# First DFT stage in float32 instead of split F32R, and the biases as one wide product

## The chip, the cores and the metric

The kernel runs on one core of a Trainium2 chip. The metric is the device time of one execution in microseconds. TensorE (PE) does the matrix products, with its weight loads shown as an engine of their own (PEld); VectorE (DVE), ScalarE (ACT) and GpSimd (POOL) do the elementwise work; SyncE (SP) issues the DMAs.

## The reference

The input x is 8 x 3072 x 256. A real Fourier transform over the 3072 positions is followed by a complex linear layer with biases, a soft threshold of 0.01 and the inverse transform; then a two-layer MLP and a routed layer of experts.

```python
X = np.fft.rfft(x, axis=1)                      # 3072 = 96 x 32
Xr, Xi = X.real, X.imag
Yr = Xr @ w_r - Xi @ w_i + b_r
Yi = Xr @ w_i + Xi @ w_r + b_i
Y  = soft(Yr, 0.01) + 1j * soft(Yi, 0.01)
y  = np.fft.irfft(Y, n=3072, axis=1)
h  = np.maximum(y @ w_in, 0.0)                  # 256 -> 2048
z  = h * h @ w_out                              # 2048 -> 256
# softmax routing of the 24576 tokens to 32 slots, 8 experts, and back
```

## The kernel before

The kernel has three parts: the spectrum (transform, linear layer, threshold and the first half of the inverse transform), some 600 us; the MLP with the second half of the inverse transform and the routing beside it, nearly all of the rest; and the experts with the recombination, the last 200 us. Products that need more precision than one F32R product gives split both factors into an upper part and a remainder and add three F32R products (`mm3`, L127 to L130: upper by upper L128, upper by lower L129, lower by upper L130).

The transform is done as 96 x 32. The first stage (`a_...`) multiplies by the 96 x 96 matrix `f1t`. Its input is loaded in tiles `xt` of 96 x 4 x 256 (`load_x`, L193, 64 in all, `XB` of them at a time). A half tile j (512 columns, 16 per batch, 128 in all) is cast to its upper part `xh` by ScalarE (`a_hi`, L199), its remainder `xl` is taken by VectorE (`a_lo`, L204; four of the first 16 by GpSimd), and `a_mm` adds three products in a bank psA. `a_out` (L222) copies the bank to `sa`, and one DMA for each tile stores it in `ad` in DRAM (L224). `load_b` (L231) reads it back as `bt` for two units.

A unit u (12 per batch, 96 in all) is one step of the rest: `b_mm` (second transform stage, four float32 products of 128 columns into psB, L239), `b_hi`, `b_lo` and `b_sum` (upper parts, remainders and the sum `Sf` of real and imaginary part), `l_mm` (linear layer), `l_move`, `l_relu` and `l_soft` (the bank read out and the threshold), `c_mm` (first inverse stage, two float32 products of 256 columns into psC, L321) and `c_out` (copy and four stores to `zd`, L327 to L331). `l_mm` fills one bank psL: for the real and the imaginary half (256 columns each) two `mm3` of 128 x 128 by 256 columns, and then one bias product, which closes that half's sum:

```python
nc.tensor.matmul(p[:, c], lhsT=sel[:, c + (c and first)], rhs=bias, start=False, stop=True)   # L290
```

`bias` is 64 x 256 with b_i and b_r in rows 0 and 1 and their remainders in rows 32 and 33, all else zero; `sel` (64 x 3 x 128) selects the row for the half. In the first unit of a batch the imaginary half has two more `mm3`. Then two `mm3` of the common part fill a bank psS.

The order is written by hand: the loop runs over half steps h, two per unit, and the steps of several units lie in each half step, so that every engine's queue has a fixed order. In an even half step TensorE gets `b_mm(U)`, `l_mm(U-2)` and then a first-stage product; in an odd one `c_mm(U-4)` and then a first-stage product. One half tile is taken in each of the first 20 half steps and in two of three afterwards, until the batches are through (from some 506 us on there are none). `a_mm(j-2)`, `a_hi(j)`, `a_lo(j-1)` and `a_out(j-3)` belong to the same half step. All PSUM banks of this part are one pool of eight, taken in turn (`pbank`). The decoding of the MLP's weights takes a step in each half step on VectorE, ScalarE and GpSimd. All loads and stores of this part are issued on SP's queue in program order.

The first batch's 16 half tiles run alone in an opening; its stores, the constants and the loads of the first units follow, and the units begin at 32 us.

Of the kernel before, what the change touches and what calls it, by code (L numbers as in the profile page):

```python
# [10 lines left out]
F32 = mybir.dt.float32  # L11
# [22 lines left out]
def shape_constants():  # L34
    """DFT factors and selection matrices: they depend on the shapes alone.

    n = 32 n1 + n2, k = k1 + 96 k2.  A row k1 of a real first-stage spectrum is
    held as (c, h, p): c = re / im, k1 = p + 24 h; the im row of k1 = 0 holds
    the real row k1 = 48.  The second stage keeps, for k >= 1536, the conjugate.
    """  # L40
# [38 lines left out]
    # rows n2 = 8 t + c of a first inverse stage, kept as (c, t)  # L79
# [15 lines left out]
    # which of the rows (b_i, b_r; 32 on: their lower parts) goes where: real part, imaginary part, the  # L95
    # latter where slot 0 holds the real k = 1536
    sel = np.zeros((64, 3, 128))
    for r in (0, 32):
        sel[r + 1, 0] = 1.0
        sel[r, 1] = 1.0  # L100
        sel[r, 2, 1:] = 1.0
        sel[r + 1, 2, 0] = 1.0
# [12 lines left out]
def fft_moe_kernel(ctx, tc, x, w_r, w_i, b_r, b_i, moe_w_in, moe_w_out, moe2_phi, moe2_w1, moe2_w2,  # L115
# [39 lines left out]
    # Both MLP products are cut in pairs of 128 hidden units.  The first takes 7 products of blocks in  # L155
    # place of 8 (Strassen's in Winograd's form): A = w_in^T of a pair, B = two blocks of tokens.
# [7 lines left out]
    f1t = k1p.tile([N1, 2, N1], F32R, tag="f1t", name="f1t")  # L164
    f1h, f1l = f1t[:, 0], f1t[:, 1]
    bm = k1p.tile([128, NP, 128], F32, tag="bm", name="bm")
    cm = k1p.tile([128, NP, 128], F32, tag="cm", name="cm")
    # w_r, -(w_r + w_i), w_i - w_r
    lwh = [k1p.tile([128, 2, DM], F32R, tag=f"lwh{j}", name=f"lwh{j}") for j in range(3)]
    lwl = [k1p.tile([128, 2, DM], F32R, tag=f"lwl{j}", name=f"lwl{j}") for j in range(3)]  # L170
    bias = k1p.tile([64, DM], F32R, tag="bias", name="bias")
    sel = k1p.tile([64, 3, 128], F32R, tag="sel", name="sel")
# [6 lines left out]
    # ---------------- spectrum, complex linear layer, shrinkage, half of the way back: all batches  # L179
# [16 lines left out]
    def a_hi(j):  # L196
        load_x(j // 2)
        xh = wka.tile([N1, 2, DM], F32R, tag="xh", name=f"xh{j}", bufs=XS)
        nc.scalar.copy(xh, xt[j // 2][:, 2 * (j % 2):2 * (j % 2) + 2])  # L199
        xs[j] = [xh]  # L200

    def a_lo(j, eng):
        xl = wka.tile([N1, 2, DM], F32R, tag="xl", name=f"xl{j}", bufs=XS - 1)
        eng.tensor_tensor(out=xl, in0=xt[j // 2][:, 2 * (j % 2):2 * (j % 2) + 2], in1=f(xs[j][0]), op=ALU.subtract)  # L204
        if j % 2:
            xt.pop(j // 2)
            load_x(j // 2 + XB)
        xs[j].append(xl)

    def a_mm(j):  # L210
        if j % NA == 0:
            ad[j // NA] = dram.tile([N1, N2, DM], F32, tag="ad", name=f"ad{j // NA}", bufs=3)
        xh, xl = xs.pop(j)
        p = pbank(f"psA{j}")[:N1].rearrange("p (a d) -> p a d", a=2)
        mm3(p, f1h, f1l, xh, xl, True, True)
        pa[j] = p
# [34 lines left out]
    def b_lo(u):  # L251
        p = pb.pop(u)
        xh, xi = xb.pop(u)
        xl = wkb.tile([128, 2, 2, 128], F32R, tag="Xl", name=f"Xl{u}")
        sf = wkb.tile([128, 2, 128], F32, tag="Sf", name=f"Sf{u}", bufs=1)
        nc.vector.tensor_tensor(out=xl, in0=p, in1=f(xh), op=ALU.subtract)
        nc.vector.tensor_tensor(out=sf, in0=p[:, :, 0], in1=xi, op=ALU.add)
        if u % NU == 0:
            # k = 0 and k = 1536 share a slot: both are real
            dd = wkb.tile([128, 2, 1], F32, tag="dd", name=f"dd{u}")  # L260
            nc.vector.tensor_tensor(out=dd, in0=xi[:, :, 0:1], in1=p[:, :, 0, 0:1], op=ALU.subtract)
            nc.vector.tensor_copy(d0h[:, :, 0:1], dd)
            nc.vector.tensor_tensor(out=d0l[:, :, 0:1], in0=dd, in1=f(d0h[:, :, 0:1]), op=ALU.subtract)
            nc.vector.tensor_copy(sf[:, :, 0:1], p[:, :, 0, 0:1])
            nc.vector.tensor_copy(xh[:, :, :, 0:1], zero)
            nc.vector.tensor_copy(xl[:, :, :, 0:1], zero)
        sp[u] = [xh, xl, sf]
# [8 lines left out]
    def l_mm(u):  # L276
        """X_im times -(w_r + w_i) for the real part, X_re times w_i - w_r for the other; both with the biases.

        Then what the two share, (X_re + X_im) w_r.
        """  # L280
        xh, xl, h, l = sp.pop(u)
        first = u % NU == 0
        p = pbank(f"psL{u}").rearrange("p (c d) -> p c d", c=2)
        for c in range(2):
            for dh in range(2):
                mm3(p[:, c], xh[:, dh, 1 - c], xl[:, dh, 1 - c], lwh[1 + c][:, dh], lwl[1 + c][:, dh], dh == 0, False)
            if c == 1 and first:
                for dh in range(2):
                    mm3(p[:, c], d0h[:, dh], d0l[:, dh], lwh[0][:, dh], lwl[0][:, dh], False, False)
            nc.tensor.matmul(p[:, c], lhsT=sel[:, c + (c and first)], rhs=bias, start=False, stop=True)  # L290
# [5 lines left out]
    def l_move(u):  # L296
        """Slots (l, h, k2) x (c, d) to (c, h, k2) x (l, d)."""
# [35 lines left out]
    # the MLP's weights: float64 decoded to float32 from its bits, then parts of 12 bits  # L333
# [5 lines left out]
    def decode():  # L339
        """The weights of a pair of hidden tiles at a time; yields after a few instructions."""  # L340
# [13 lines left out]
        for n, (k, q, a) in enumerate(keys):  # L354
# [4 lines left out]
            if wide:  # L359
# [7 lines left out]
                # +-2^e; 1 + the fraction's upper 20 bits; its other 32 bits  # L367
# [23 lines left out]
            # A11, A12, S4, -A22; S1, S2, S3  # L391
# [14 lines left out]
    # ---------------- rest of the way back, MLP, routing of tokens  # L406
# [10 lines left out]
    def stage_d(s, bank):  # L417
        """B11, B21, B12, B22 of two blocks of tokens and the sums of these that the products take."""
# [41 lines left out]
    XB, XS, XL, SA = 5, 5, NC, 4  # L460
    with tc.manual_schedule():
# [4 lines left out]
        f1f = wka.tile([N1, N1], F32, tag="f1f", name="f1f", bufs=1)  # L466
        nc.sync.dma_start(f1f, c_f1)
        for j in range(XB):
            load_x(j)
        split(f1h, f1l, f1f)  # L470
        w_ri = [wka.tile([128, 2, DM], F32, tag=f"wri{k}", name=f"wri{k}", bufs=1) for k in range(2)]
        bs = wka.tile([2, DM], F32, tag="bs", name="bs", bufs=1)
        sf = wka.tile([64, 3, 128], F32, tag="sf", name="sf", bufs=1)
        for j in range(NA + 4):
            if j < NA:
                a_hi(j)
                a_lo(j, nc.gpsimd if j in (2, 5, 8, 11) else nc.vector)
            if 1 <= j <= NA:
                a_mm(j - 1)
            if j >= 4:  # L480
                a_out(j - 4, nc.scalar.copy if j % 2 else nc.vector.tensor_copy)
            if j == NA - 4:
                for t, v in zip(w_ri, (w_r, w_i)):
                    nc.sync.dma_start(t, v.rearrange("(a p) n -> p a n", p=128))
                nc.sync.dma_start(bs[0:1], b_i.rearrange("(o n) -> o n", o=1))
                nc.sync.dma_start(bs[1:2], b_r.rearrange("(o n) -> o n", o=1))
                nc.sync.dma_start(sf, c_se)
# [4 lines left out]
        nc.vector.tensor_copy(bias, zero[:64, 0, 0].broadcast_to([64, DM]))  # L492
# [7 lines left out]
        nc.scalar.copy(bias[0:2], bs)  # L500
        nc.vector.tensor_tensor(out=bias[32:34], in0=bs, in1=f(bias[0:2]), op=ALU.subtract)
# [6 lines left out]
        XB, XS, XL, SA = 2, 3, NB * NC, 2  # L508
# [17 lines left out]
        for h in range(2 * NT + 12):  # L526
            U, o = divmod(h, 2)
            # the first stage of the batches to come
            j = -1
            if (h < 20 or (h + 1) * 2 // 3 > h * 2 // 3) and aj < NB * NA + 3:  # L530
                j, aj = aj, aj + 1
            def first_stage():
                if NA <= j - 2 < NB * NA:
                    a_mm(j - 2)
                if NA <= j < NB * NA:
                    a_hi(j)
                if j >= NA + 3:
                    a_out(j - 3, nc.scalar.copy)

            if o == 0:  # L540
# [3 lines left out]
                if NA <= j - 1 < NB * NA:  # L544
                    a_lo(j - 1, nc.vector)
# [4 lines left out]
            else:  # L550
                at(U - 4, c_mm)
                at(U - 2, l_move)
                if NA <= j - 1 < NB * NA:
                    a_lo(j - 1, nc.vector)
# [52 lines left out]
        class Unit:  # L607
            """A pair of hidden tiles for two blocks of tokens."""
# [7 lines left out]
            def product(self, p, j, start):  # L616
                """One of the seven, on its own or onto a sum that may have been read."""
# [7 lines left out]
            def copy(self, tag):  # L625
                """What the sum of products holds so far."""
# [14 lines left out]
            def hi(self, k):  # L641
                """The upper part of the square: of the square, or from what was cut at zero."""
# [22 lines left out]
            def second(self, k):  # L665
                """Hidden tile k // 2 of the pair, block k % 2 of the tokens."""
# [18 lines left out]
        def small(shape, tag, i):  # L685
            """The last block's route runs beside the one before it, and takes what tokens no longer need."""
# [81 lines left out]
        # the experts' weights go where those of the MLP were  # L768
# [30 lines left out]
        # the softmax over tokens, from the parts that the partitions hold  # L799
# [30 lines left out]
        # what goes beside the products: slots of a superblock at which each of these takes a step  # L830
# [91 lines left out]
    # ---------------- slots through the experts, tokens from the slots  # L922
    with ExitStack() as p3:
# [12 lines left out]
        # how the tokens combine the slots: 8 blocks at a time, in two parts  # L936
# [93 lines left out]
def device_arrays(inputs):  # L1030
    """The inputs as they come; a float64 array as its raw bits."""
# [24 lines left out]
```

## Time and profile before

| | us |
|---|---|
| median of 3 runs | 2992.5 (2991.92 to 2994.35) |
| span of the profiled execution, first to last instruction | 2989.6 |
| what the median has beyond that span | 2.9 |
| TensorE busy | 2946.6 (99%) |
| VectorE busy | 2271.9 (76%) |
| ScalarE busy | 1787.9 (60%) |
| GpSimd busy | 241.4 (8%) |

The page gives the span of the profiled execution and not its device time. A matmul is pipelined and its end is modelled, so its slot is read from its start to the start of the next one, not from its length. L12 is line 12 of the kernel. A row of the timeline merges neighbours of one kind (x4: four instructions). A program's float32 product can show as more than one record.

### The profile page before, as it was taken

How to read it: one execution, taken by the hardware profiler on the slowest of the kernel's cores; microseconds unless marked ns; L12 is line 12 of the kernel's file. 1: busy time of each engine (PE TensorE's matmuls, PEld its weight loads, DVE VectorE, ACT ScalarE, POOL GpSimd, SP SyncE). 2: the span in 40 equal slices, each digit the busy share in tenths (PEclk: the TensorE clock that was granted, in tenths of full speed). 3: DMA queues.
4: the chain of work that ended last, by engine and by line, in shares of the span. 5: the costliest groups of instructions: out<-in, count | busy, mean ns of one | idle time of the engine just before them, and what ended most of it. 6: DMA issues, size and time to landing. Idle time of an engine off the chain costs nothing.

```text
span 2989.6 us, 50050 instructions
## 1 busy us (share of the span) xinstructions
PE 2946.6 (99%) x18382; PEld 2752.5 (92%) x18382; DVE 2271.9 (76%) x5077; ACT 1787.9 (60%) x4137; POOL 241.4 (8%) x274
## 2 busy tenths in 40 slices
PE   7999999999999999999999999999999999999988
PEld 5888888899999999999999999999999999999967
DVE  6888888677777777777777777777777777777745
ACT  5777777555555555565555656555555555555532
POOL 1344344100000000000000000000000000000021
PEclk9999999999999999999999999999999999999999
DMA  8777766310000000000000000000000000000269
GB/s 247 205 203 197 202 196 182 93 33 11 15 16 14 17 14 12 14 12 14 11 14 12 14 12 14 12 14 14 12 14 17 14 14 17 12 14 1 74 213 325
DMA packets 125737, 189.85 MB, mean 64 GB/s; under 512 B 15346, under 2 KB 98100, under 8 KB 125236
## 3 DMA queue, kind: packets, MB, share of 16 engines
q1 hardware_dynamic: 123700, 183.51, 21.2%
q10 hardware_dynamic: 1792, 3.15, 0.4%
q8 instruction: 145, 2.38, 0.3%
q14 instruction: 100, 0.82, 0.1%
HBM read 107.95 MB, written 78.64 MB: 62 GB/s over the span
## 4 chain that ended last, share of the span: by engine, by line
PE 94%; DMA 2%; DVE 2%; ACT 1%; SPq 1%; issue 1%; POOL 0%; ACTq 0%; POOLq 0%; DVEq 0%
PE psA L622 18%; PE psX L622 13%; PE psO L130 12%; PE psO L129 12%; PE psO L128 12%; PE psY L427 4%; PE psB L239 3%; PE psC L321 3%; PE psL L128 2%; PE psL L290 2%; PE psL L129 1%; PE psL L130 1%; PE psS L128 1%; PE pz L756 1%; PE pl L702 1%; PE psA L129 1%
## 5 line engine op out<-in xcount | busy, mean ns | idle before, releaser
L130 PE MATMUL psO<-gh,wo 128*128 128x384 f32 x2048 | 685.6, 335 | 0.0
L129 PE MATMUL psO<-gl,wo 128*128 128x384 f32 x2048 | 684.7, 334 | 0.0
L128 PE MATMUL psO<-gh,wo 128*128 128x384 f32 x2048 | 684.7, 334 | 0.0
L662 DVE TENSOR_TENSOR gl<-g,gh 128x384 fp32r<-128x384 f32 x1024 | 554.9, 551 | 77.4 <-ACT gh L645 73.4
L645 ACT CAST gh<-g 128x384 fp32r<-128x384 f32 x512 | 263.4, 515 | 401.9 <-DVE g L654 400.6
L129 PEld LDWEIGHTS psO<-gl,wo 128*128 128x128 f32 x2048 | 384.5, 188 | 0.1
L128 PEld LDWEIGHTS psO<-gh,wo 128*128 128x128 f32 x2048 | 384.5, 188 | 0.0
L130 PEld LDWEIGHTS psO<-gh,wo 128*128 128x128 f32 x2048 | 384.5, 188 | 0.0
L622 PE MATMUL psA<-yh,wib 128*128 128x384 f32 x1024 | 360.0, 352 | 1.2 <-ACT r L628 1.2
L622 PE MATMUL psA<-yh,wia 128*128 128x384 f32 x1024 | 360.9, 352 | 0.0
L622 PE MATMUL psX<-yh,wia 128*128 128x384 f32 x1024 | 344.6, 337 | 0.1
L654 DVE SCALAR_TENSOR_TENSOR g<-h 128x384 f32<-128x384 f32 x512 | 281.8, 550 | 0.1
L633 DVE TENSOR_TENSOR h<-psX,W 128x384 f32<-128x384 f32 x256 | 142.7, 557 | 174.4 <-ACT W L628 172.7
L633 DVE TENSOR_TENSOR h<-psX,r 128x384 f32<-128x384 f32 x256 | 142.5, 557 | 162.2 <-PE psX L622 113.9
L656 DVE TENSOR_TENSOR g<-r 128x384 f32<-128x384 f32 x512 | 260.2, 550 | 0.0
L628 ACT COPY W<-psA 128x384 f32<-128x384 f32 x256 | 122.6, 479 | 207.0 <-PE psA L622 207.0
L647 ACT ACTIVATE gh<-r 128x384 fp32r<-128x384 f32 x512 | 240.7, 518 | 8.1
L305 DVE TENSOR_TENSOR ub<-psL,st 64x256 f32<-64x256 f32 x384 | 161.8, 421 | 84.2 <-ACT st L301 80.1
L633 DVE TENSOR_TENSOR h<-psX,V 128x384 f32<-128x384 f32 x256 | 142.2, 555 | 107.6 <-PE psX L622 104.8
L628 ACT COPY r<-psA 128x384 f32<-128x384 f32 x256 | 122.6, 479 | 166.7 <-PE psA L622 133.4
L628 ACT COPY V<-psA 128x384 f32<-128x384 f32 x256 | 122.6, 479 | 146.6 <-PE psA L622 144.2
L622 PEld LDWEIGHTS psA<-yh,wib 128*128 128x128 f32 x1024 | 194.0, 189 | 7.9 <-ACT gh L647 6.1
(235 smaller groups left out, 6261.6 us busy)
## 6 DMA issues: line engine op xcount, KB each, us to landing
xt<-in_x_dram SPq DMA_DIRECT2D x64, 384.0 KB, 3.9
ad<-sa SPq DMA_DIRECT2D x64, 384.0 KB, 4.4
bt<-ad SPq DMA_DIRECT2D x192, 128.0 KB, 3.8
zd<-sc SPq DMA_DIRECT2D x384, 64.0 KB, 3.1
zt<-zd SPq DMA_DIRECT2D x64, 384.0 KB, 3.5
out_dram<-ob SPq DMA_DIRECT2D x64, 384.0 KB, 3.4
w<-in_moe_w_dram SPq DMA_DIRECT2D x5, 1024.0 KB, 10.6
raw<-in_moe_w_in_dram SPq DMA_DIRECT2D x16, 256.0 KB, 3.7
```

The costliest lines, as they stand in the source:

```text
L128: nc.tensor.matmul(o, lhsT=ah, rhs=bh, start=start, stop=False)
L129: nc.tensor.matmul(o, lhsT=ah, rhs=bl, start=False, stop=False)
L130: nc.tensor.matmul(o, lhsT=al, rhs=bh, start=False, stop=stop)
L305: nc.vector.tensor_tensor(out=ub[64 * c:64 * c + 64, l], in0=p[s, c], in1=st[s], op=ALU.add)
L622: nc.tensor.matmul(p, lhsT=w[:, k, l], rhs=r[:, j], start=start and n == 0, stop=n == 2, skip_group_check=True)
L628: nc.scalar.copy(t, self.a)
L633: nc.vector.tensor_tensor(out=h, in0=self.x, in1=t, op=ALU.add)
L645: nc.scalar.copy(h, self.g[k][0])
L647: nc.scalar.activation(out=h, in_=self.g[k][0], func=AF.Square)
L654: nc.vector.scalar_tensor_tensor(out=g, in0=t, scalar=0.0, in1=t, op0=ALU.max, op1=ALU.mult)
L656: nc.vector.tensor_tensor(out=g, in0=t, in1=t, op=ALU.mult)
L662: nc.vector.tensor_tensor(out=l, in0=g, in1=f(h), op=ALU.subtract)
```

## The change

The first stage's factor stays in float32 (`f1t` is loaded as it is, 96 x 96), and `a_mm` is one float32 product of `f1t` with the loaded half tile, 512 columns. The upper parts and remainders (`a_hi`, `a_lo`, and the split of `f1t`) go. `a_mm(j)` and `a_out(j-1)` belong to a half step now, in place of `a_mm(j-2)` and `a_out(j-3)`, and in the opening `a_out` follows `a_mm` by two half tiles. `xt` has six buffers in place of five in the opening, and three in place of two afterwards; the load into a buffer that comes free is issued behind `a_mm` of the tile's second half.

The biases become one product of 128 rows and 512 columns per unit, issued first in the bank: it begins the sum of both halves, and the other products add to it. `bias` is 128 x 512: row 0 holds b_i in the imaginary half, rows 1 and 2 hold b_r in the real and in the imaginary half, rows 32 to 34 their remainders; the rest is zero. `sel` is 128 x 2 x 128.

```diff
-        sel[r + 1, 0] = 1.0
-        sel[r, 1] = 1.0
-        sel[r, 2, 1:] = 1.0
-        sel[r + 1, 2, 0] = 1.0
+        sel[r, 0] = 1.0
+        sel[r + 1] = 1.0
+        sel[r, 1, 1:] = 1.0
+        sel[r + 2, 1, 0] = 1.0
...
-    f1t = k1p.tile([N1, 2, N1], F32R, tag="f1t", name="f1t")
-    f1h, f1l = f1t[:, 0], f1t[:, 1]
+    f1t = k1p.tile([N1, N1], F32, tag="f1t", name="f1t")
...
-    bias = k1p.tile([64, DM], F32R, tag="bias", name="bias")
-    sel = k1p.tile([64, 3, 128], F32R, tag="sel", name="sel")
+    bias = k1p.tile([128, 2 * DM], F32R, tag="bias", name="bias")
+    sel = k1p.tile([128, 2, 128], F32R, tag="sel", name="sel")
...
-    def a_hi(j):
+    def a_mm(j):
+        if j % NA == 0:
+            ad[j // NA] = dram.tile([N1, N2, DM], F32, tag="ad", name=f"ad{j // NA}", bufs=3)
         load_x(j // 2)
-        xh = wka.tile([N1, 2, DM], F32R, tag="xh", name=f"xh{j}", bufs=XS)
-        nc.scalar.copy(xh, xt[j // 2][:, 2 * (j % 2):2 * (j % 2) + 2])
...
-        eng.tensor_tensor(out=xl, in0=xt[j // 2][:, 2 * (j % 2):2 * (j % 2) + 2], in1=f(xs[j][0]), op=ALU.subtract)
+        p = pbank(f"psA{j}")[:N1].rearrange("p (a d) -> p a d", a=2)
+        nc.tensor.matmul(p, lhsT=f1t, rhs=xt[j // 2][:, 2 * (j % 2):2 * (j % 2) + 2], start=True, stop=True)
+        pa[j] = p
         if j % 2:
             xt.pop(j // 2)
             load_x(j // 2 + XB)
...
-        mm3(p, f1h, f1l, xh, xl, True, True)
...
-        p = pbank(f"psL{u}").rearrange("p (c d) -> p c d", c=2)
+        p = pbank(f"psL{u}")
+        nc.tensor.matmul(p, lhsT=sel[:, int(first)], rhs=bias, start=True, stop=False, skip_group_check=True)
+        p = p.rearrange("p (c d) -> p c d", c=2)
...
-            nc.tensor.matmul(p[:, c], lhsT=sel[:, c + (c and first)], rhs=bias, start=False, stop=True)
...
-    XB, XS, XL, SA = 5, 5, NC, 4
+    XB, XL, SA = 6, NC, 4
...
-        bs = wka.tile([2, DM], F32, tag="bs", name="bs", bufs=1)
-        sf = wka.tile([64, 3, 128], F32, tag="sf", name="sf", bufs=1)
-        for j in range(NA + 4):
+        bs = wka.tile([3, 2, DM], F32, tag="bs", name="bs", bufs=1)
+        sf = wka.tile([128, 2, 128], F32, tag="sf", name="sf", bufs=1)
+        nc.vector.memset(bs, 0.0)
+        for j in range(NA + 2):
             if j < NA:
-                a_hi(j)
-                a_lo(j, nc.gpsimd if j in (2, 5, 8, 11) else nc.vector)
-            if 1 <= j <= NA:
-                a_mm(j - 1)
-            if j >= 4:
-                a_out(j - 4, nc.scalar.copy if j % 2 else nc.vector.tensor_copy)
+                a_mm(j)
+            if j >= 2:
+                a_out(j - 2, nc.scalar.copy if j % 2 else nc.vector.tensor_copy)
...
-                nc.sync.dma_start(bs[0:1], b_i.rearrange("(o n) -> o n", o=1))
-                nc.sync.dma_start(bs[1:2], b_r.rearrange("(o n) -> o n", o=1))
+                for r, c, v in ((0, 1, b_i), (1, 0, b_r), (2, 1, b_r)):
+                    nc.sync.dma_start(bs[r:r + 1, c], v.rearrange("(o n) -> o n", o=1))
...
-        XB, XS, XL, SA = 2, 3, NB * NC, 2
+        XB, XL, SA = 3, NB * NC, 2
...
-                if NA <= j - 2 < NB * NA:
-                    a_mm(j - 2)
                 if NA <= j < NB * NA:
-                    a_hi(j)
-                if j >= NA + 3:
-                    a_out(j - 3, nc.scalar.copy)
+                    a_mm(j)
+                if j >= NA + 1:
+                    a_out(j - 1, nc.scalar.copy)
...
-                if NA <= j - 1 < NB * NA:
-                    a_lo(j - 1, nc.vector)
```

## Rows read from the trace of the kernel before

**Rows 1.** Page, part 1: busy us (share of the span) x instructions

```profile
PE 2946.6 (99%) x18382; PEld 2752.5 (92%) x18382; DVE 2271.9 (76%) x5077; ACT 1787.9 (60%) x4137; POOL 241.4 (8%) x274
```

**Rows 2.** Page, part 4: the chain that ended last, shares by engine

```profile
PE 94%; DMA 2%; DVE 2%; ACT 1%; SPq 1%; issue 1%; POOL 0%; ACTq 0%; POOLq 0%; DVEq 0%
```

**Rows 3.** Window: busy (count) of PE, PEld, DVE, ACT, POOL; clock; DMA, GB/s

```profile
110.00:520.00 410.00, 409.30 (x2550) 347.02 (x2548) 350.18 (x731) 309.93 (x715) 175.28 (x198) 1.00 0.70 195
```

**Rows 4.** Waits of PE, 50 to 560 us: total us, times, longest

```profile
PE psB L239 <- DVE Sf L257: 0.7, 1, 0.7
```

**Rows 5.** Groups by line, 0 to 700 us: busy us, mean ns, idle before

```profile
L204 DVE TENSOR_TENSOR xl<-xt,xh 96x512 fp32r<-96x512 f32 x124 | 100.7, 815 | 17.1 <-ACT xh L199 15.4
L199 ACT CAST xh<-xt 96x512 fp32r<-96x512 f32 x128 | 79.7, 630 | 18.3 <-DMA xt<-in_x_dram 18.2
...
L321 PE MATMUL psC<-ub,cm 128*128 128x256 f32 x384 | 100.8, 385 | 3.2 <-DVE ub L315 3.2
...
L290 PE MATMUL psL<-bias,sel 64*128 64x256 f32 x192 | 73.3, 382 | 0.0
```

**Rows 6.** Timeline of PE around one bias product: start us, us, instruction

```profile
302.50 0.28 PE L129 MATMUL psL<-lwl,Xh 128*128 128x256 f32 x1
302.61 0.28 PE L130 MATMUL psL<-lwh,Xl 128*128 128x256 f32 x1
302.82 0.38 PE L290 MATMUL psL<-bias,sel 64*128 64x256 f32 x1
303.13 0.39 PE L128 MATMUL psL<-lwh,Xh 128*128 128x256 f32 x1
303.35 0.28 PE L129 MATMUL psL<-lwl,Xh 128*128 128x256 f32 x1
```

**Rows 7.** Timeline of the weight loads, same stretch

```profile
302.50 0.19 PEld L130 LDWEIGHTS psL<-lwh,Xl 128*128 128x128 f32 x1
302.81 0.18 PEld L290 LDWEIGHTS psL<-bias,sel 64*128 64x128 f32 x1
303.13 0.19 PEld L128 LDWEIGHTS psL<-lwh,Xh 128*128 128x128 f32 x1
```

**Rows 8.** Timeline of PE, 305 to 308 us: first stage, float32 products

```profile
305.38 0.40 PE L129 MATMUL psA<-xl,f1t 96*96 96x512 f32 x1
305.61 0.39 PE L130 MATMUL psA<-xh,f1t 96*96 96x512 f32 x1
305.85 1.03 PE L321 MATMUL psC<-ub,cm 128*128 128x256 f32 x4
306.71 1.05 PE L239 MATMUL psB<-bm,bt 128*128 128x128 f32 x8
307.52 0.36 PE L128 MATMUL psL<-lwh,Xh 128*128 128x256 f32 x1
```

**Rows 9.** Timeline of ACT in the opening

```profile
5.44 1.14 ACT L199 CAST xh<-xt 96x512 fp32r<-96x512 f32 x2 [2.58 <-DMA xt<-in_x_dram]
...
21.00 0.58 ACT L222 COPY sa<-psA 96x512 f32<-96x512 f32 x1 [1.26 <-PE psA L130]
```

**Rows 10.** Timeline of PE in the opening

```profile
7.37 0.63 PE L130 MATMUL psA<-xh,f1t 96*96 96x512 f32 x1
7.80 0.63 PE L128 MATMUL psA<-xh,f1t 96*96 96x512 f32 x1
...
11.64 0.39 PE L128 MATMUL psA<-xh,f1t 96*96 96x512 f32 x1
...
20.54 0.39 PE L130 MATMUL psA<-xh,f1t 96*96 96x512 f32 x1
```

**Rows 11.** Waits of SP's queue, 40 to 560 us

```profile
SPq L193 <- DVE xl L204: 105.2, 47, 4.7
```

**Rows 12.** Timeline of DVE late in the stage, units without first-stage products

```profile
577.97 1.73 DVE L305 TENSOR_TENSOR ub<-psL,st 64x256 f32<-64x256 f32 x4 [2.28 <-ACT st L301]
...
582.86 1.73 DVE L305 TENSOR_TENSOR ub<-psL,st 64x256 f32<-64x256 f32 x4 [1.39 <-ACT st L301]
```

More of the change, by code (lines that the diff above doesn't have):

```diff
@@ L94, in shape_constants @@
     f = np.float32
-    sel = np.zeros((64, 3, 128))
+    sel = np.zeros((128, 2, 128))
     for r in (0, 32):
-        sel[r + 1, 0] = 1.0
-        sel[r, 1] = 1.0
-        sel[r, 2, 1:] = 1.0
-        sel[r + 1, 2, 0] = 1.0
+        sel[r, 0] = 1.0
+        sel[r + 1] = 1.0
+        sel[r, 1, 1:] = 1.0
+        sel[r + 2, 1, 0] = 1.0
     return {
@@ L194, in load_x @@
         xt[c] = t
-    def a_hi(j):
+    def a_mm(j):
+        if j % NA == 0:
+            ad[j // NA] = dram.tile([N1, N2, DM], F32, tag="ad", name=f"ad{j // NA}", bufs=3)
         load_x(j // 2)
-        xh = wka.tile([N1, 2, DM], F32R, tag="xh", name=f"xh{j}", bufs=XS)
-        nc.scalar.copy(xh, xt[j // 2][:, 2 * (j % 2):2 * (j % 2) + 2])
-        xs[j] = [xh]
-    def a_lo(j, eng):
-        xl = wka.tile([N1, 2, DM], F32R, tag="xl", name=f"xl{j}", bufs=XS - 1)
-        eng.tensor_tensor(out=xl, in0=xt[j // 2][:, 2 * (j % 2):2 * (j % 2) + 2], in1=f(xs[j][0]), op=ALU.subtract)
+        p = pbank(f"psA{j}")[:N1].rearrange("p (a d) -> p a d", a=2)
+        nc.tensor.matmul(p, lhsT=f1t, rhs=xt[j // 2][:, 2 * (j % 2):2 * (j % 2) + 2], start=True, stop=True)
+        pa[j] = p
         if j % 2:
@@ L207, in a_lo @@
             load_x(j // 2 + XB)
[L208 to L214, printed above, removed]
-        mm3(p, f1h, f1l, xh, xl, True, True)
-        pa[j] = p
     def a_out(j, copy):
@@ L282, in l_mm, with on @@
         first = u % NU == 0
-        p = pbank(f"psL{u}").rearrange("p (c d) -> p c d", c=2)
+        p = pbank(f"psL{u}")
+        nc.tensor.matmul(p, lhsT=sel[:, int(first)], rhs=bias, start=True, stop=False, skip_group_check=True)
+        p = p.rearrange("p (c d) -> p c d", c=2)
+        def on(o, ah, al, w, stop):
+            for x, y, last in ((ah, lwh, False), (ah, lwl, False), (al, lwh, stop)):
+                nc.tensor.matmul(o, lhsT=x, rhs=y[w[0]][:, w[1]], start=False, stop=last, skip_group_check=True)
         for c in range(2):
             for dh in range(2):
[L286 to L289, printed above, removed]
-            nc.tensor.matmul(p[:, c], lhsT=sel[:, c + (c and first)], rhs=bias, start=False, stop=True)
+                on(p[:, c], xh[:, dh, 1 - c], xl[:, dh, 1 - c], (1 + c, dh), c == 1 and dh == 1 and not first)
+        if first:
+            for dh in range(2):
+                on(p[:, 1], d0h[:, dh], d0l[:, dh], (0, dh), dh == 1)
         s = pbank(f"psS{u}")[:, :DM]
@@ L465, in fft_moe_kernel @@
         wka = p0.enter_context(tc.tile_pool(name="wka0", bufs=2))
-        f1f = wka.tile([N1, N1], F32, tag="f1f", name="f1f", bufs=1)
-        nc.sync.dma_start(f1f, c_f1)
+        nc.sync.dma_start(f1t, c_f1)
         for j in range(XB):
             load_x(j)
-        split(f1h, f1l, f1f)
         w_ri = [wka.tile([128, 2, DM], F32, tag=f"wri{k}", name=f"wri{k}", bufs=1) for k in range(2)]
-        bs = wka.tile([2, DM], F32, tag="bs", name="bs", bufs=1)
-        sf = wka.tile([64, 3, 128], F32, tag="sf", name="sf", bufs=1)
-        for j in range(NA + 4):
+        bs = wka.tile([3, 2, DM], F32, tag="bs", name="bs", bufs=1)
+        sf = wka.tile([128, 2, 128], F32, tag="sf", name="sf", bufs=1)
+        nc.vector.memset(bs, 0.0)
+        for j in range(NA + 2):
             if j < NA:
-                a_hi(j)
-                a_lo(j, nc.gpsimd if j in (2, 5, 8, 11) else nc.vector)
-            if 1 <= j <= NA:
-                a_mm(j - 1)
-            if j >= 4:
-                a_out(j - 4, nc.scalar.copy if j % 2 else nc.vector.tensor_copy)
+                a_mm(j)
+            if j >= 2:
+                a_out(j - 2, nc.scalar.copy if j % 2 else nc.vector.tensor_copy)
             if j == NA - 4:
@@ L491, in fft_moe_kernel @@
             nc.vector.tensor_copy(t, zero[:, :, 0, :].broadcast_to([128, 2, 128]))
-        nc.vector.tensor_copy(bias, zero[:64, 0, 0].broadcast_to([64, DM]))
+        nc.vector.tensor_copy(bias, zero[:, 0, 0].broadcast_to([128, 2 * DM]))
         wr, wi = w_ri
@@ L499, in fft_moe_kernel @@
         nc.scalar.copy(sel, sf)
-        nc.scalar.copy(bias[0:2], bs)
-        nc.vector.tensor_tensor(out=bias[32:34], in0=bs, in1=f(bias[0:2]), op=ALU.subtract)
+        bs = bs.rearrange("p c d -> p (c d)")
+        nc.scalar.copy(bias[0:3], bs)
+        nc.vector.tensor_tensor(out=bias[32:35], in0=bs, in1=f(bias[0:3]), op=ALU.subtract)
         p0.close()
@@ L529, in fft_moe_kernel @@
             j = -1
-            if (h < 20 or (h + 1) * 2 // 3 > h * 2 // 3) and aj < NB * NA + 3:
+            if (h < 20 or (h + 1) * 2 // 3 > h * 2 // 3) and aj < NB * NA + 1:
                 j, aj = aj, aj + 1
             def first_stage():
-                if NA <= j - 2 < NB * NA:
-                    a_mm(j - 2)
                 if NA <= j < NB * NA:
-                    a_hi(j)
-                if j >= NA + 3:
-                    a_out(j - 3, nc.scalar.copy)
+                    a_mm(j)
+                if j >= NA + 1:
+                    a_out(j - 1, nc.scalar.copy)
             if o == 0:
@@ L552, in fft_moe_kernel @@
                 at(U - 2, l_move)
-                if NA <= j - 1 < NB * NA:
-                    a_lo(j - 1, nc.vector)
                 at(U, b_hi)
```

## The prediction, made before the change was run

> **What bounds the kernel now.** I read four views in this order. The page's first part gives TensorE as busy for nearly the whole span [rows 1]; alone that proves little, because a matmul's end is modelled. The chain of work that ended last settles it: 94% of it is TensorE's own instructions following one another, and no other engine has more than 2% [rows 2]. The change touches only the spectrum stage (the first 600 us), so I then read that stage alone: between 110 and 520 us TensorE is without work for 0.7 of 410 us at the full granted clock, while VectorE and ScalarE have about 60 and 100 us free [rows 3]. Last, the waits: between 50 and 560 us TensorE waited for another engine once, for 0.7 us [rows 4]. So this stage takes as long as its products occupy TensorE, and what is cut from or added to a slot there (from one product's start to the next one's) moves everything behind it, the MLP too, which is bound in the same way. An edit on VectorE or ScalarE is worth nothing by itself here.
>
> **The first stage.** Before, each of the 128 half tiles cost a cast on ScalarE (79.7 us in all) and a subtraction, 124 of them on VectorE (100.7 us) [rows 5], then three F32R products. Casts and subtractions go; since TensorE did not wait for them, their saving is put at nothing. On TensorE, three F32R products of 512 columns, 0.23 us from start to start [rows 8], take 0.69 us. The float32 product that replaces them has no 512-wide row, but narrower ones do. The 192 float32 products of c_mm (two for each of 96 units) show as 384 records [rows 5], and the four of b_mm in a unit as eight [rows 8]: two records each. Four c_mm records of 256 columns fill the 0.86 us from 305.85 to 306.71, 0.215 us each; eight b_mm records of 128 columns fill 0.81 us, 0.10 each [rows 8]. The cost grows with the columns. A 512-wide float32 product is then two records of 0.43 us, 0.86 us; by the b_mm rows it would be 8 x 0.10 = 0.81. I take 0.86, as the 256-wide rows are nearer. That makes the edit a loss of 0.17 us on each product: 112 of the 128 lie in the pipelined part (16 stand in the opening), so 112 x 0.17 = +19.0 us (+13.4 at 0.81). The two weight loads are of 96 columns and lie beside 0.43 us records; 128-column loads take 0.19 us [rows 7].
>
> **The biases.** This is where the time is. In the timeline of TensorE's products, the starts around one bias product are 302.61 (the last product of a run), 302.82 (bias), 303.13 (next) and 303.35 (the one behind): 0.74 us for three slots [rows 6]. Within a run the products of 256 columns start 0.11 us apart (302.50 to 302.61, [rows 6]), and half of the 512-wide 0.23 is 0.115, which I take; without the bias two slots would be 0.23. One bias product costs 0.51 us, though it has the columns of a 0.115 us product. The weight loads say why: every other load is issued a product ahead (302.50 for the product at 302.61), but the bias's load starts at 302.81, 0.01 us before its product, and the next run's load at 303.13, with its product [rows 6, 7]. The array is drained on both sides. What differs about it is its shape: 64 rows among 128-row products; the 128-row c_mm follows a 96-row product at the usual 0.24 us [rows 8]. Two per unit and 96 units make 192 [rows 5]: 192 x 0.51 = 97.9 us.
>
> The Trainium skill's page "TensorE: Matmul & The Clock Gate" (section "Why this matters for your kernels") says a matmul of few rows takes the same time as one of 128, and (section "LDWEIGHTS (loading the stationary operand)") that load time follows columns, not rows. The load's own duration here agrees (0.18 beside 0.19 us), the slot doesn't; by that page making the product taller would gain nothing.
>
> After the change there is one product of 128 rows and 512 columns per unit. Its nearest row in width is the 512-wide F32R product, 0.23 us [rows 8]; the upper end is today's drained slot widened by 256 columns, 0.51 + 0.115 = 0.63. I take 0.23, because nothing with the full array's shape shows the drain in [rows 6 to 8]. Being first of the bank it follows the float32 b_mm, a place that today's first product of the run holds, so that change of type is paid already. Saving: 1.02 - 0.23 = 0.79 us per unit, 96 x 0.79 = 75.8 us (37.4 at 0.63).
>
> **What is moved.** a_mm no longer waits for a cast but for the load of xt itself, with b_mm or c_mm of the next half step queued behind it on TensorE. The load is given three tiles of lead in place of two, six half tiles at no more than one in each half step of 2.4 us [rows 12], some 14 us; the very first tile was there 5.4 us into the span [rows 9]. SP's queue waits for TensorE where it waited for VectorE's subtraction, 105.2 us in 47 waits now [rows 11]; behind it are stores of the spectrum and the loads of later units, which have half steps to spare: nothing. In the opening TensorE can start at 5.4, when the first tile is there, without the cast behind it (two in 1.14 us, [rows 9]). At 1.2 GHz (0.43 us per 512 columns, 7.37 to 7.80 [rows 10]) a float32 product takes 1.72 us. If the clock reaches 2.4 GHz 4.3 us after dense work begins, as it did from 7.37 to 11.64 (the record falls from 0.63 to 0.39 us, [rows 10]), 2.5 products are done by 9.7 and the other 13.5 take 11.6: the last ends near 21.4, against 20.9 now (20.54 + 0.39, [rows 10]), behind which the copy at 21.00 and the store stand [rows 9]. I put +0.5 us, between -1 (the earlier start, and the clock up sooner) and +12 (all sixteen at 1.2 GHz: 13.5 x 0.86 more). The bias rows' casts and zeroing are on engines that then wait for the store; one small bias DMA more on SP's queue stands ahead of stores that wait for copies anyway: nothing. When the units begin, first-stage products come two half tiles ahead of where they stood: work put earlier, 0, between -2 and +2.
>
> **Sum.** 2989.6 (span) + 19.0 - 75.8 + 0.5 = 2933.3 us. The profiled execution's own time is not listed; the median, 2992.5, lies 2.9 above the span, so I forecast 2936 us.
>
> **Rivals.** (1) The drain isn't due to the 64 rows but to the bias product as such; then one is left in place of two, at 0.63 us: -37.4 + 19.0 + 0.5, 2975 us. For it: I have only one shape of bias product. Against: the loads of all 128-row and 96-row products run ahead. The page's rule points this way; read literally (0.115 per bias product now) it would give no saving and 3012, which [rows 6] exclude. Chance 7%.
> (2) With units 0.6 to 0.8 us shorter, another engine's loop sets the pace: the eight PSUM banks go round, and psB must be read by VectorE (Sf) before its bank returns; the one wait of [rows 4] is of this kind. For it: units without a first-stage product shrink from 4.9 (577.97 to 582.86, [rows 12]) to 4.1 us with no relief on VectorE. Against: there VectorE sits idle 1.39 us or more before one step of each unit [rows 12], and elsewhere it is rid of 0.8 us per half tile (100.7 / 124, [rows 5]). At 0.2 us for each of 96 units: +19, 2955 us. Chance 10%.
> (3) Slower: a float32 product of the full 512 columns costs more than in proportion, say four records (two passes over two halves), 1.72 us. Then 112 x 1.03 = +115 - 75.8 + 14 in the opening: 3046 us. It decides from 0.69 + 75.8/112 = 1.37 us on. Against: 128 and 256 columns are in proportion. Chance 3%.
> (4) The float32 product is cheaper than I take it and the opening gains: 2929, within the forecast's own range.
>
> **How the numbers follow.** Forecast as worked out 77%, rivals 7, 10 and 3%, and 3% for what I haven't thought of. Its own range: 0.81 against 0.86 (-6), the opening and the units' beginning (-3 to +12): 2927 to 2948; beats read to 0.01 us (192 x 0.01, 2 us) lie within. As some of the forecast's 77% may fall out of that, I reach to rival 2: 2927 to 2956. A measurement of this kernel can tell about 0.2% (6 us): faster by more than that in the forecast and rivals 1 and 2, 0.94; within it 0.02 and slower 0.04, which are rival 3 and the rest.
>
> **What would show it.** In the profile after: the bias product once per unit, its load issued ahead or right after b_mm and the next product 0.23 us (not 0.6) later; psA as two records 0.43 us apart; units of 4.1 us without and 5.0 with one first-stage product; TensorE still at no waits. Waits of psB or psS for VectorE would be rival 2; four psA records, rival 3. A bias slot near 0.6 us would make my reading of the drain wrong.

## The result, and the profile after

The changed kernel takes 2940.0 us in the median of four runs (2937.4 to 2941.7), against 2992.6 for the kernel before: a ratio of 0.9824, with a 95% interval of 0.981 to 0.9838. The forecast was 2936 us with a range of 2927 to 2956. The profiled execution took 2940.89 us, 1.8 us more than its span.

The page of the changed kernel, parts 1 (busy time by engine) and 4 (the chain that ended last, by engine), beside [rows 1, 2]:

```profile
PE 2893.7 (98%) x18158; PEld 2702.4 (92%) x18158; DVE 2182.8 (74%) x4953; ACT 1720.4 (59%) x4008; POOL 217.8 (7%) x270
PE 95%; DMA 2%; DVE 1%; ACT 1%; SPq 0%; issue 0%; POOL 0%; ACTq 0%; POOLq 0%; DVEq 0%
```

TensorE bounds the kernel as before, and the 50.5 us that the span lost (2989.6 to 2939.1) are TensorE's: 52.9 us of its busy time. The sum of the prediction went from the span to the median with 2.9 us, as before; here the median lies 0.9 above the profiled span, so the median misses the forecast by 4 us and the span by 5.8.

The timeline of TensorE's products in the changed kernel, where one unit passes to the next (start us, us, instruction), beside [rows 6, 8]:

```profile
301.21 0.28 PE L130 MATMUL psS<-lwh,Sl 128*128 128x256 f32 x1
301.33 1.02 PE L200 MATMUL psA<-xt,f1t 96*96 96x512 f32 x2
302.19 1.03 PE L315 MATMUL psC<-ub,cm 128*128 128x256 f32 x4
303.06 1.05 PE L227 MATMUL psB<-bm,bt 128*128 128x128 f32 x8
303.87 0.48 PE L272 MATMUL psL<-bias,sel 128*128 128x512 f32 x1
304.19 0.28 PE L277 MATMUL psL<-lwh,Xh 128*128 128x256 f32 x1
304.31 0.28 PE L277 MATMUL psL<-lwl,Xh 128*128 128x256 f32 x1
```

The float32 first-stage product is two records, and from its start to c_mm's it takes 0.86 us (301.33 to 302.19). The bias product's slot is 0.32 us (303.87 to 304.19). Before, the first product of the run stood in this place and had a slot of 0.20 us (307.52 of [rows 8] to 307.72 behind it in the same timeline) instead of its usual 0.12. The product behind b_mm pays these 0.08 us in either kernel, so the bias product itself costs about 0.24.

The weight loads of the same stretch, beside [rows 7]:

```profile
303.84 0.19 PEld L272 LDWEIGHTS psL<-bias,sel 128*128 128x128 f32 x1
303.95 0.19 PEld L277 LDWEIGHTS psL<-lwh,Xh 128*128 128x128 f32 x1
304.19 0.19 PEld L277 LDWEIGHTS psL<-lwl,Xh 128*128 128x128 f32 x1
```

The load of the product behind the bias now starts at 303.95, 0.24 us before that product (304.19) and beside the bias product. The gap on that side is gone.

The commonest length of a unit, from the first psS product of one unit to that of the next in the timelines, for eight of the kernels (us):

| kernel | no first-stage product | one | two | median time |
|---|---|---|---|---|
| before | 4.89 | 5.57 | 6.26 | 2992.6 |
| after | 4.07 | 4.99 | 5.85 | 2940.0 |
| e1: bias change alone | 4.11 | 4.81, many longer | 5.53, many longer | 2943.8 |
| e2: first stage alone | 4.89 | 5.74 | 6.61 | 3009.9 |
| e3: two bias products, 128 rows | 4.13 | 4.98 | 5.84 | 2939.5 |
| e4: one bias product, 64 rows | 4.51 | 5.33 | 6.19 | 2972.2 |
| e10: one bias product, 96 rows | 4.13 | 4.97 | 5.81 | 2937.5 |
| e11: two of 64 rows, back to back | 4.51 | 5.34 | 6.20 | 2973.6 |

The three largest waits of TensorE in the changed kernel up to 640 us (total us, times, longest), beside [rows 4], which began at 50 us:

```profile
PE psB L227 <- DMA bt<-ad: 11.3, 1, 11.3
PE psA L200 <- DMA xt<-in_x_dram: 7.5, 2, 5.5
PE psC L315 <- DVE ub L309: 4.9, 3, 3.2
```

The first two are the opening and the beginning of the units. The third is partly new: besides one wait of 3.2 us at the end of the stage (2.7 before), TensorE waits for VectorE at 479 us, where units without first-stage products meet steps of the weights' decoding. From the timelines of VectorE, GpSimd and TensorE there:

```profile
472.82 0.69 DVE L309 SCALAR_TENSOR_TENSOR ub<-ub,ua 128x512 f32<-128x512 f32 x1
...
477.29 0.42 DVE L371 SCALAR_TENSOR_TENSOR ex<-raw,ex 128x256 int32<-128x256 int32 x1
477.63 1.22 DVE L309 SCALAR_TENSOR_TENSOR ub<-ub,ua 128x512 f32<-128x512 f32 x1
...
477.35 0.95 POOL L373 TENSOR_TENSOR mh<-mh,d 128x256 f32<-128x256 f32 x1
...
479.00 1.10 PE L315 MATMUL psC<-ub,cm 128*128 128x256 f32 x4 [0.82 <-DVE ub L309]
```

VectorE is busy for 15.6 of the 16 us from 476 to 492. Part of that is a longer operation: `ub` (L309) takes 1.22, 1.18 and 1.14 us in the three units there and 0.69 in the units around them, each time while GpSimd runs a product of the decoding (L373, L375). Not every such overlap in the trace lengthens it.

### The profile page after: what moved, and what is told of

Same layout as the page of the kernel before. It is cut to its first block, busy times and chain, and to the rows that moved or that the text cites. A ratio compares the mean times of both kernels' runs of the same rounds, so it can differ in the third digit from the quotient of the medians.

```text
span 2939.1 us, 49214 instructions
## 1 busy us (share of the span) xinstructions
PE 2893.7 (98%) x18158; PEld 2702.4 (92%) x18158; DVE 2182.8 (74%) x4953; ACT 1720.4 (59%) x4008; POOL 217.8 (7%) x270
## 3 DMA queue, kind: packets, MB, share of 16 engines
q10 hardware_dynamic: 1792, 3.15, 0.4%
## 4 chain that ended last, share of the span: by engine, by line
PE 95%; DMA 2%; DVE 1%; ACT 1%; SPq 0%; issue 0%; POOL 0%; ACTq 0%; POOLq 0%; DVEq 0%
PE psA L607 19%; PE psX L607 14%; PE psO L130 12%; PE psO L128 12%; PE psO L129 12%; PE psL L277 5%; PE psA L200 4%; PE psY L421 4%; PE psB L227 3%; PE psC L315 3%; PE pz L741 1%; PE pl L687 1%; PE px L701 1%; DMA out_dram<-ob 1%; PE psS L129 1%; PE psS L130 1%
```

## The experiments

Two theories stood against each other: that the 64 rows of the bias product make TensorE drain on both sides, and that the product costs this as such, by its place or by being there. Besides, the prediction took it that work removed from VectorE is worth nothing.

**e3: the old two products, with 128 rows.** On the changed kernel, `l_mm` and the bias tile are as before the change, but padded with zero rows (lines against the kernel before):

```diff
-    bias = k1p.tile([64, DM], F32R, tag="bias", name="bias")
-    sel = k1p.tile([64, 3, 128], F32R, tag="sel", name="sel")
+    bias = k1p.tile([128, DM], F32R, tag="bias", name="bias")
+    sel = k1p.tile([128, 3, 128], F32R, tag="sel", name="sel")
```

> The same, but bias and sel have 128 rows (the added ones zero), still two products of 256 columns, each closing its half. If the 64 rows cause the drain, the slots are 0.115 us each, and the time is that of the changed kernel, 2940 us within 4. If it comes from the product's place or from its being there at all: 0.51 each, 3015 us.

It took 2939.5 us (2938.5 to 2941.6), the time of the changed kernel. Its products and weight loads around one bias product:

```profile
301.87 0.28 PE L130 MATMUL psL<-lwh,Xl 128*128 128x256 f32 x1
301.98 0.28 PE L278 MATMUL psL<-bias,sel 128*128 128x256 f32 x1
302.10 0.28 PE L128 MATMUL psL<-lwh,Xh 128*128 128x256 f32 x1
302.22 0.28 PE L129 MATMUL psL<-lwl,Xh 128*128 128x256 f32 x1
...
301.87 0.19 PEld L278 LDWEIGHTS psL<-bias,sel 128*128 128x128 f32 x1
```

Same place, same count, same columns as in [rows 6]; the three slots take 0.35 us instead of 0.74, and the load runs a product ahead. The rows are the cause. Making one wide product of the two, and putting it first, brought nothing measurable beyond that.

**e4: the new single product, with 64 rows.**

```diff
-    bias = k1p.tile([128, 2 * DM], F32R, tag="bias", name="bias")
-    sel = k1p.tile([128, 2, 128], F32R, tag="sel", name="sel")
+    bias = k1p.tile([64, 2 * DM], F32R, tag="bias", name="bias")
+    sel = k1p.tile([64, 2, 128], F32R, tag="sel", name="sel")
```

> The changed kernel with 64 rows in bias and sel: one product of 512 columns first in the bank. If the 64 rows cause the drain: 0.28 to 0.51 us per unit more (one side of it is there anyway behind the float32 b_mm), 2967 to 2989 us. If rows don't matter: 2940 us.

2972.2 us (2971.3 to 2973.0): 32 us more than with 128 rows, 0.34 us in each of 96 units. Products, then weight loads:

```profile
301.43 1.05 PE L227 MATMUL psB<-bm,bt 128*128 128x128 f32 x8
302.42 0.50 PE L272 MATMUL psL<-bias,sel 64*128 64x512 f32 x1
302.84 0.39 PE L277 MATMUL psL<-lwh,Xh 128*128 128x256 f32 x1
303.07 0.28 PE L277 MATMUL psL<-lwl,Xh 128*128 128x256 f32 x1
...
302.41 0.18 PEld L272 LDWEIGHTS psL<-bias,sel 64*128 64x128 f32 x1
302.84 0.19 PEld L277 LDWEIGHTS psL<-lwh,Xh 128*128 128x128 f32 x1 [0.25 <-issue]
```

b_mm's slot grows from 0.81 (303.06 to 303.87 after) to 0.99 us, the bias's from 0.32 to 0.42, and the next one's from 0.12 to 0.23; the load behind the bias starts with its product again. The three slots are 0.39 us longer together, the units 0.34 to 0.44.

**e11: the two 64-row products back to back**, at the end of the bank, with the first stage in float32. (The lines are against the `l_mm` of before. The bank's second half is begun while its first is still open, and its sums are not those of the reference; the products, their shapes and their number are as described.)

```diff
         for c in range(2):
             for dh in range(2):
                 ...
-            nc.tensor.matmul(p[:, c], lhsT=sel[:, c + (c and first)], rhs=bias, start=False, stop=True)
+        for c in range(2):
+            nc.tensor.matmul(p[:, c], lhsT=sel[:, c + (c and first)], rhs=bias, start=False, stop=True, skip_group_check=True)
```

> The first stage in float32 and the biases as two 64-row products of 256 columns as before, but one behind the other at the end of the bank instead of one at the end of each half. If the price is paid for each change between 64 and 128 rows, one pair of changes is left: 0.39 us a unit less than the 3010 us with the products apart, 2973 us. If each 64-row product drains the array by itself: 3010.

2973.6 us (2972.6 to 2974.3), 36 less than with the products apart (e2). Products:

```profile
299.86 0.28 PE L274 MATMUL psL<-lwh,Xl 128*128 128x256 f32 x1
300.07 0.50 PE L284 MATMUL psL<-bias,sel 64*128 64x256 f32 x2
300.50 0.39 PE L128 MATMUL psS<-lwh,Sh 128*128 128x256 f32 x1
300.73 0.28 PE L129 MATMUL psS<-lwl,Sh 128*128 128x256 f32 x1
```

From 299.86 to 300.73 four slots take 0.87 us; one bias product made three slots of 0.74. The second 64-row product adds 0.13 us. What is paid for is the change from 128 to 64 rows and back, about 0.4 us for such a pair of changes, and not the product.

**e10: 96 rows** in the changed kernel's `bias` and `sel`.

> The changed kernel with 96 rows in bias and sel in place of 128. The 96-row products of the first stage stood among 128-row ones without a drain; if it is only the step to 64 rows that drains: 2940 us within 4. If every change in the number of rows drains when the product is followed by a 128-row one with weights of 128 columns: as with 64 rows, 2972.

2937.5 us (2936.8 to 2938.6): as with 128.

```profile
302.50 0.48 PE L272 MATMUL psL<-bias,sel 96*128 96x512 f32 x1
302.81 0.28 PE L277 MATMUL psL<-lwh,Xh 128*128 128x256 f32 x1
302.93 0.28 PE L277 MATMUL psL<-lwl,Xh 128*128 128x256 f32 x1
```

So it isn't any difference in rows, and 128 is not needed. The Trainium skill's page "TensorEngine Tiling (Array Packing)" (sections "Tiling Modes" and "Key Properties") lists 64 x 128 as a configuration of its own beside 128 x 128 and says that changing the mode drains TensorE. Five runs agree with that: 64 rows show the longer slots and late loads (e2, e4), 96 and 128 do not (e10, e3), and two 64-row products in a row pay once (e11). The traces show slots and loads, not the mode; that the 64-row product is run in that configuration is inferred. The sentence of the Trainium skill's page "TensorE: Matmul & The Clock Gate" that the prediction weighed, that few rows take the same time, agrees with the product alone (0.13 us for e11's second one, beside 0.115) and leaves the change of mode out.

**e8: no bias product.**

```diff
-        nc.tensor.matmul(p, lhsT=sel[:, int(first)], rhs=bias, start=True, stop=False, skip_group_check=True)
```

> The changed kernel without the bias product (the biases are left out of the result). Its price by the prediction is 0.23 us in each of 96 units: 22 us less, 2918 us, with units 0.23 us shorter. If the product still drains the array on one side, 0.3 to 0.4 us a unit: 2902 to 2911.

2920.3 us (2918.3 to 2921.0), 19.7 us less, 0.2 us a unit; units of 3.85, 4.71 and 5.60 us, 0.22 to 0.28 shorter each. The product costs no more than its columns, and TensorE also begins to wait for VectorE at times (6.9 us, 3.4 of them the wait at the stage's end).

**e2: the first stage alone.** The changed kernel with the biases as before.

> The changed kernel with the biases as before: two 64-row products of 256 columns closing the halves. By the prediction's terms 19 us more than before in the pipelined part, and 0.5 to 5 in the opening: 3012 to 3017 us. If the first stage in float32 gave something by relieving VectorE and ScalarE it would lie under 3005.

3009.9 us (3008.6 to 3013.0), ratio 1.0059 (1.0044 to 1.0074): slower. Against before, units with one first-stage product grow from 5.57 to 5.74 us and with two from 6.26 to 6.61, 0.17 to 0.18 for each product, forecast 0.17; units without one stay at 4.89. The time lies 2 us under the range expected, but not under the 3005 that would have shown a gain from relieving VectorE.

**e1: the bias change alone.** The kernel before, with the changed bias tile and `l_mm` and nothing else.

> The kernel before with the new bias product alone; the first stage stays three F32R products. If TensorE stays the bound of the stage: 75.8 us less than before, 2917 us, faster than the changed kernel, with units 0.79 us shorter than before in each kind (4.1, 4.8, 5.5). Rival: VectorE takes over. Its work is 350 us in the 410 us from 110 to 520, 5.0 us for a mean unit of 5.83, and TensorE would need 5.04; then units stretch where decoding steps fall, TensorE shows waits for VectorE, and the time lies at 2922 to 2942.

2943.8 us (2942.6 to 2945.6): 49 us faster than before and not 76, and 2 us above the range expected for the rival too. Its commonest units are about as long as the sum says (4.81, 5.53), but many are longer, up to 7.65. Busy time from 110 to 450 us (columns as in [rows 3]) and the longest of TensorE's waits there:

```profile
110.00:450.00 340.00, 328.38 (x2235) 293.69 (x2234) 321.59 (x662) 280.48 (x655) 150.79 (x174) 1.00 0.77 217
PE psC L327 <- DVE ub L321: 5.2, 10, 1.0
PE psA L128 <- DVE Sf L257: 3.2, 5, 1.0
PE psB L239 <- DVE Sf L257: 2.6, 4, 1.0
```

TensorE is without work for 11.6 of 340 us and VectorE is busy for 95%. The next three runs ask whether VectorE's subtractions are the cause.

**e9: no remainders.** As e1, but a tile of zeros in place of each remainder in the units' part.

```diff
-        xl = wka.tile([N1, 2, DM], F32R, tag="xl", name=f"xl{j}", bufs=XS - 1)
-        eng.tensor_tensor(out=xl, in0=xt[j // 2][:, 2 * (j % 2):2 * (j % 2) + 2], in1=f(xs[j][0]), op=ALU.subtract)
+        xl = cur["xl0"]
```

> The kernel before with the new bias product and three F32R products, but in the units' part the remainder of a half tile is not computed: a tile of zeros stands in its place (that part of the product is left out of the result). TensorE's work is that of the bias change alone, VectorE is rid of all 112 subtractions, GpSimd gets nothing. If VectorE's subtractions kept the bias change alone at 2944 us: TensorE's own sum, 2917 to 2922 us. If the loop over the banks or the DMAs did: 2935 or more.

2923.1 us (2921.7 to 2925.2), 21 us less than e1, a little above the upper end expected. The same window:

```profile
110.00:450.00 340.00, 339.85 (x2360) 311.77 (x2359) 265.69 (x609) 292.83 (x687) 151.60 (x186) 1.00 0.80 225
```

VectorE falls to 78%, TensorE has work all the time, and nearly all units have the lengths of e1's commonest ones. TensorE's products are the same in both, so VectorE's subtractions hold e1 up. TensorE's waits there are for VectorE's results (`ub`) and for banks that VectorE reads late (`Sf`); the DMAs are not the limit (they move more here, 225 beside 217 GB/s).

**e6: float32 for every second half tile.** As e1, with one float32 product for odd half tiles of the units' part and three F32R products for even ones.

```diff
+    def plain(j):
+        return j >= NA and j % 2
...
+        if plain(j):
+            nc.tensor.matmul(p, lhsT=f1f, rhs=xt[j // 2][:, 2 * (j % 2):2 * (j % 2) + 2], start=True, stop=True)
+            next_x(j)
+        else:
+            xh, xl = xs.pop(j)
+            mm3(p, f1h, f1l, xh, xl, True, True)
...
-        XB, XS, XL, SA = 2, 3, NB * NC, 2
+        XB, XS, XL, SA = 3, 2, NB * NC, 2
```

> The new bias product, and a first stage that is one float32 product for every second half tile of the pipelined part (56 of 112) and three F32R products for the others. TensorE's own sum: 2992.6 - 75.8 + 56 x 0.17 = 2926 us; VectorE is rid of 45 us, about 295 of 355 us. If VectorE's load is the cause: 2926 to 2934 us, better than either half of the change. If the float32 products were what cost the changed kernel its last microseconds by another way, nearer to 2940.

2935.0 us (2932.2 to 2938.7), ratio 0.9809 (0.9796 to 0.9823). The same window, and TensorE's one kind of wait in it:

```profile
110.00:450.00 340.00, 337.57 (x2238) 293.98 (x2237) 294.17 (x634) 266.11 (x625) 150.86 (x176) 1.00 0.82 219
PE psA L128 <- DVE Sf L272: 2.2, 3, 1.0
```

With VectorE at 87% TensorE loses 2.4 us. The time is 1 us above the range expected for VectorE's load as the cause. This is the fastest of the kernels that compute the whole, 5 us below the changed kernel in the medians; the two intervals of the ratio overlap, so the lead isn't settled.

**e5: half of the remainders on GpSimd.** As e1, with one changed argument in both half steps:

```diff
-                    a_lo(j - 1, nc.vector)
+                    a_lo(j - 1, nc.gpsimd if j % 2 else nc.vector)
```

> The kernel before with the new bias product, first stage in three F32R products, and the remainders of every second half tile taken by GpSimd instead of VectorE (56 of the 112, some 45 us off VectorE, some 80 us onto GpSimd at 1.4 us each). If VectorE's load was what held the bias change alone at 2944 us: back towards TensorE's own sum, 2917 to 2930 us. If it was something else (the chain from bank to bank, the DMAs): 2944 again. If the two engines get in each other's way: no better than 2935.

2948.7 us (2943.8 to 2951.4), no better than e1. Groups of VectorE from 110 to 450 us (busy us, mean ns, idle before), first e1's, then e5's, and e5's largest wait of TensorE:

```profile
L204 DVE TENSOR_TENSOR xl<-xt,xh 96x512 fp32r<-96x512 f32 x84 | 71.6, 852 | 1.3
L374 DVE TENSOR_SCALAR ex<-raw 128x256 int32<-128x256 int32 x27 | 11.3, 418 | 1.8 <-POOL v L387 1.7
...
L204 DVE TENSOR_TENSOR xl<-xt,xh 96x512 fp32r<-96x512 f32 x42 | 39.5, 940 | 0.7
L374 DVE TENSOR_SCALAR ex<-raw 128x256 int32<-128x256 int32 x27 | 18.3, 679 | 4.7 <-POOL v L387 4.5
...
PE psC L327 <- DVE ub L321: 9.8, 10, 1.8
```

VectorE loses half of its subtractions, but the rest grow from 852 to 940 ns, a decoding step from 418 to 679, and its waits for GpSimd's product from 1.7 to 4.5 us. TensorE loses 12.2 of 340 us, as in e1. Whether the longer operations or the waits in VectorE's queue cost more is not separated.

**e7: the first stage two half tiles later**, as before the change.

```diff
-                if NA <= j < NB * NA:
-                    a_mm(j)
-                if j >= NA + 1:
-                    a_out(j - 1, nc.scalar.copy)
+                if NA <= j - 2 < NB * NA:
+                    a_mm(j - 2)
+                if j >= NA + 3:
+                    a_out(j - 3, nc.scalar.copy)
```

> The changed kernel with a_mm(j-2) and a_out(j-3) in place of a_mm(j) and a_out(j-1): the first stage of the units' part stands two half tiles later, as before the change. If the later first linear layer after the restart comes from the products ahead of it: 1 to 3 us less, 2937 to 2939. If it comes from the opening and the clock: no change, 2940.

2939.2 us (2937.5 to 2939.9), 0.8 less than the changed kernel, inside the scatter of both: where the products stand at the units' beginning doesn't matter.

## Why the prediction was right, point by point

**What bounds the kernel.** Right: TensorE's slots set the time before and after.

**First stage, +0.17 us for each product.** Right to the hundredth: the 0.86 us extrapolated from 256 columns is the slot measured, and e2 shows 0.17 for each product. "Their saving is put at nothing" holds for the kernel before, where TensorE had the longer queue, but not beside the other half of the change. Without the float32 stage the bias change would have given 49 us (e1), because VectorE's subtractions become the bound. The part that I booked as a pure loss of 19 us is slower alone (e2: +17 us) and some 4 us faster on top of the bias change (2943.8 to 2940.0; the runs of the two don't overlap, the intervals of their ratios do). The terms are not independent: the sum came out because both parts were made at once, and adding e1's gain and e2's loss gives 2961.

**The biases, -75.8 us.** Right in cause, and in size to some 6 us. Cause: the rows, by e3, e4, e10 and e11. Size: the new product costs about 0.24 us against 0.23 forecast; units without a first-stage product shrink by 0.82 us, those with one by 0.58 (0.79 - 0.17 = 0.62 forecast). From e2 to the changed kernel, the bias part alone gives 3009.9 - 2940.0 = 70 us; with the 2.3 us of waits for VectorE below, 72.

**Where 5.8 us of the span went.** The sum gave 2933.3, the span was 2939.1. Up to the first psS product the changed kernel took 3.15 us longer (47.81 against 44.66). The sum has 1.8 for that stretch: 0.5 in the opening, four first-stage products at 0.86 in place of two at 0.69, less the first unit's 0.79. So 1.4 are missing there, and they lie in the opening, where the first unit's product starts at 33.94 instead of 31.93 us: +2.0 against +0.5 forecast. In this profile the faster clock came later than the sum has it. The weight loads show it, 0.28 us long at 1.2 GHz and 0.16 at 2.4:

```profile
5.54 17.09 PE L200 MATMUL psA<-xt,f1t 96*96 96x512 f32 x32 [5.54 <-DMA xt<-in_x_dram]
33.94 2.05 PE L227 MATMUL psB<-bm,bt 128*128 128x128 f32 x8 [11.31 <-DMA bt<-ad]
...
11.59 0.28 PEld L200 LDWEIGHTS psA<-xt,f1t 96*96 96x96 f32 x1 [0.57 <-issue]
12.17 0.16 PEld L200 LDWEIGHTS psA<-xt,f1t 96*96 96x96 f32 x1 [0.29 <-issue]
```

The first product had started at 5.54, so the first short load came 6.6 us behind it; the 4.3 us that I took from [rows 10] were too few. Part of that is a wrong reading: I counted from 7.37, but the products before had begun at 6.11, 5.5 us before 11.64.

```profile
6.11 0.74 PE L128 MATMUL psA<-xh,f1t 96*96 96x512 f32 x1 [6.11 <-ACT xh L199]
31.93 3.74 PE L239 MATMUL psB<-bm,bt 128*128 128x128 f32 x16 [11.01 <-DMA bt<-ad]
```

The size of this term isn't settled by one profile of either kernel. Seven other kernels have the same 32 records in the opening (e2, e3, e4, e7, e8, e10, e11), and in their profiles the first short load comes 4 to 7 us after the first product and the first unit's product starts between 31.59 and 33.54 us. In e1, e5, e6 and e9, which have the old opening, it starts at 32.8 to 33.3. The earliest is e3's:

```profile
31.59 2.05 PE L227 MATMUL psB<-bm,bt 128*128 128x128 f32 x8 [10.51 <-DMA bt<-ad]
...
8.63 0.28 PEld L200 LDWEIGHTS psA<-xt,f1t 96*96 96x96 f32 x1 [0.57 <-issue]
9.32 0.16 PEld L200 LDWEIGHTS psA<-xt,f1t 96*96 96x96 f32 x1 [0.41 <-issue]
```

The forecast's +0.5 lies inside that spread; that the change itself lengthens the opening is not shown.

The other 95 units gave 55.3 us (546.5 to 491.2, between the first and the last psS product); 95 x 0.79 less the change from 110 products at 0.69 to 108 at 0.86 would be 58.1. Some 2.3 of the 2.8 missing lie in three units from 477.2 to 492.5 us (5.27, 4.41 and 5.57 in place of 4.07 or, for the first of a batch with its six more products, some 4.8), the waits for VectorE shown above. That is rival 2 in small: it came only where decoding steps meet units without first-stage products, 2.3 us and not 19. The rest, 1.6 us, lies behind the last psS product, in the waits at the change to the MLP.

**Rivals 1 and 3** didn't occur: the slot is near 0.3 us and not 0.6, and psA is two records. **Rival 2** was the right mechanism at the wrong price here, and the true bound of the bias change alone. The rows for it stood in [rows 3]: VectorE's 350 us in 410 are 5.0 us a unit, as much as TensorE would need after the bias change alone. I compared VectorE only with what the whole change left it.

## What to carry to other kernels

Look for products of 64 rows between products of the full array, and read their price from the starts of three neighbouring slots and from the weight load that isn't issued ahead; padding with zero rows to 96 or 128, or putting such products side by side, lowers it: in this kernel padding took away all of it, and putting two side by side left one pair of changes. Other row counts were not run. When a change has a part that cuts the bounding engine's work and a part that relieves the next engine, hold the second engine's load against the bound that the first part leaves: what is worth nothing before can be what lets the gain through. Moving work to a third engine isn't the same as removing it (e5 beside e9).

## What the runs showed that I had not expected

The opening is not the same from one profile to the next: the first psS product of the units comes at 47.8 us in the changed kernel, at 47.0 in e4, 47.4 in e10 and 47.6 in e11, but at 45.5 in e3 and 48.7 in e2, with the same first-stage products up to there. These are single profiles of different kernels, and whether the kernel or the execution makes the difference is open. But some 3 us of the time are decided before the units begin, about as much as a kernel's runs differ, so a step of that size in the opening can't be read from one profile.

A change between 64-row and 128-row products and back costs about 0.4 us, three and a half times the slot of a 256-column product (0.115 us), and shows as no wait of its products: TensorE counted as busy 409.3 of 410 us before [rows 3].
